# A new written-out order of all operations for a fused linear-attention and gated-unit kernel, planned with other prices for two of its operations

## The chip, the core and the metric

The kernel runs on one core of a Trainium2 chip. The time is that of one execution on the device, in microseconds (us); a kernel is run several times and the median is compared. A core has a matrix engine (TensorE, PE in the profile), two engines that can read TensorE's output memory PSUM (VectorE, DVE; ScalarE, ACT), a fourth engine that cannot (GpSimd, POOL), a queue engine that only issues transfers here (SyncE, SP), and 16 DMA engines. Each engine works through its own list of instructions in order and waits at an instruction until what it needs is there.

## The reference, cut to what matters

Inputs are q, k and v of 8 batches x 8 heads x 576 positions x 64, and four weights. Everything is float32 outside.

```python
def phi(x):
    proj = einsum('bhsd,df->bhsf', x, w_phi)            # 64 -> 128 features
    proj = proj - max(abs(proj), axis=-1)
    return concatenate([exp(proj), exp(-proj)], -1)
q_p, k_p = phi(q), phi(k)
kv  = einsum('bhsf,bhsd->bhfd', k_p, v);  z = sum(k_p, axis=2)
x   = einsum('bhsf,bhfd->bhsd', q_p, kv) / (einsum('bhsf,bhf->bhs', q_p, z) + 1e-6)
# x is put together to 8 x 576 x 512
gate = sigmoid(sum over 5 taps of conv_w[k] * x shifted by 4 - k positions)
out  = (gate * (x @ w_val)) @ w_out
```

## The kernel before, in words

The work is cut by batch, and a batch into small tasks. A position pair (two neighbouring positions of a head) makes a row of 128 numbers, so that a batch of q or k is 18 chunks of 128 such rows; they are treated in five units (UNITS) of 4, 4, 4, 4 and 2 chunks. For each batch:

* k and q are brought in and transposed. Batch 0 comes as float32 and is transposed on TensorE (tp32) and copied out of PSUM by DVE or ACT (tc32, lines 516 to 522). Batch 1 comes as bf16, is transposed on TensorE (tp16) and copied by DVE or ACT (tc16, lines 535 to 540). From batch 2 on the loads go out on GpSimd's queue (load) and a transposing DMA goes out on SP's (xpose, line 543). v comes on SP's queue (loadv, line 509) into two buffers that batches use in turn.
* For k: kp projects a unit into two PSUM banks, kmax (DVE, line 562) takes the absolute maximum, kexp (ACT, line 572, two per unit) writes the two exponentials. The maximum is not subtracted but goes as exp into v: ek (ACT) makes the factors and vs (GpSimd, line 588; one of 32 on DVE) scales v with them, four times per batch. st (36 matmuls each) sums k and v products, kv copies them out (DVE or ACT).
* For q: qm projects, qmax (DVE) takes maxima, mqt and mqr turn them round, qp projects again with the maximum subtracted, qexp (ACT, line 657) makes the exponentials.
* num multiplies q's features with kv, nrm (DVE, lines 688 to 691) divides, xtp and xtc (or a DMA, xtd) turn the result, halo (GpSimd) copies its rims. gate (TensorE) does the convolution, tanh (ACT) the gate, val (TensorE) the value product, gv (DVE) their product, gvc (GpSimd) collects left-over columns, out (TensorE) makes the output, oev (DVE or ACT) evicts it, odma (SP) stores it.
* Once, near the start: c_eb, c_cw, c_cw2 and c_gt make weights for the q projection and the gate. c_gt is 15 GpSimd instructions (lines 469 to 478) that need c_cw2 on DVE. hold is a tiny copy that keeps GpSimd's first loads until k of batch 0 has landed.
* warm2 is a pair of matmuls whose result nobody reads; NW says how many such tasks there are, and WARM puts in more of them as "place in the order : bank : how many".

The order around all this is written out. build makes the list of about 1,060 tasks, each with its engine or engines, a planned duration for each, and its needs. A planner outside the file made three strings out of that list, and follow (line 145) only reads them: ORDER is the order in which tasks are emitted, by their numbers in build; FLEX says, for each task that two engines could do, which one does it (A, D or P); BANKS gives each PSUM group its banks. An engine's list is the part of ORDER that is its own. The planned durations, dve and act among them, don't reach the program. The warm tasks have the numbers 1 to NW, so that with another NW all numbers behind them shift.

SP's queue holds the loads of v, the transposing DMAs and the stores in one order. In the first part it is: k and q of batch 0, v of batches 0, 1 and 2, then the transposition of k of batch 2.

Of the kernel before, what the change touches and what calls it, by code (L numbers as in the profile page):

```python
# [16 lines left out]
B, H, S, D = 8, 8, 576, 64  # L17
F = 128
DM = 512
P = 128  # L20
# [5 lines left out]
PEB = 1  # L26
XB = (6, 7)
NO = 6
NW = 14
NJ = 2 * NC  # L30
XH = R // 2
HALO = 16
XW = HALO + XH
WARM = (
    "8:7:5 21:7:1 214:5:1 "
)
STD = 1.18
E1 = D + 1
QW = 2 * NR

ORDER = (
    "15 16 18 17 20 19 22 21 24 35 23 37 26 25 36 39 57 27 38 59 41 32 34 170 40 43 61 60 33 172 55 42 73 74 64 47 171 174 58 "
    "193 311 49 63 44 0 28 76 62 56 50 29 48 65 93 75 45 94 67 53 91 66 54 30 46 92 51 68 97 173 31 89 98 77 188 90 184 52 "
    "185 95 194 96 69 186 189 72 79 5 187 99 228 2 71 100 229 104 313 190 105 70 226 80 9 106 227 101 78 1 103 234 191 110 "
    "175 235 192 10 111 230 178 102 182 179 183 107 112 231 180 108 195 312 11 181 232 109 84 233 81 197 203 82 206 196 6 85 "
    "113 83 314 204 198 8 7 114 199 12 201 319 236 237 205 86 200 320 115 238 202 207 87 210 4 88 116 239 208 315 14 240 118 "
    "117 316 209 211 119 122 212 128 317 241 129 215 242 123 217 124 318 214 125 120 130 213 176 131 243 321 216 329 121 13 "
    "332 3 322 126 331 177 127 132 218 324 330 354 433 434 219 323 355 247 221 248 435 139 220 352 140 353 250 141 436 252 "
    "358 359 149 222 251 249 325 437 150 133 327 356 134 357 244 438 135 246 360 361 223 326 245 333 224 439 136 225 328 137 "
    "265 335 362 266 142 138 363 334 337 143 145 144 338 336 151 339 367 152 440 369 146 253 340 370 254 441 368 267 268 255 "  # L50
    "341 259 442 372 269 256 261 343 260 364 371 443 262 147 366 444 342 148 450 365 446 447 263 452 154 449 445 451 166 155 "
    "257 264 562 448 563 258 458 565 167 344 459 453 347 485 564 345 461 273 346 274 486 454 460 348 455 270 275 477 478 162 "
    "456 271 566 481 457 158 482 163 479 272 480 376 159 349 377 160 483 284 484 378 156 462 350 161 464 285 373 465 351 157 "
    "276 374 567 463 277 487 286 466 488 568 375 467 279 278 492 569 287 379 493 280 153 380 288 281 468 570 494 282 289 164 "
    "573 283 571 577 575 391 472 578 295 576 299 392 165 296 574 393 572 579 290 469 685 686 394 300 606 470 580 607 395 381 "
    "688 471 495 687 382 385 473 496 307 386 497 608 308 581 383 583 609 387 303 584 388 489 304 384 689 291 491 582 389 490 "
    "292 498 604 390 499 474 605 475 500 585 476 610 588 405 611 399 406 690 400 586 410 407 401 691 396 587 411 501 397 612 "
    "503 414 692 613 398 502 589 402 415 591 614 403 693 408 590 404 615 293 592 616 409 593 297 510 618 595 301 506 511 168 "
    "412 617 507 294 696 413 622 298 699 729 812 813 516 730 302 624 425 416 169 594 517 504 623 814 426 421 698 505 518 619 "
    "422 519 815 508 621 697 599 512 429 620 513 727 816 430 509 628 596 629 520 431 728 731 600 630 597 694 625 732 598 735 "  # L60
    "432 627 514 736 417 626 515 712 733 418 695 715 601 734 714 700 602 702 713 521 603 524 703 522 817 527 523 701 525 528 "
    "530 526 818 529 531 704 532 737 705 708 819 537 711 738 707 539 538 820 709 535 706 305 540 633 710 427 536 739 423 716 "
    "533 634 309 740 722 306 631 534 741 748 428 632 856 750 745 424 935 857 541 643 746 635 936 310 644 639 723 747 636 542 "
    "937 640 749 751 645 637 646 753 938 558 543 638 647 752 823 559 717 854 862 641 826 863 939 546 855 825 724 718 642 547 "
    "860 725 861 554 726 824 742 555 858 744 719 859 827 720 743 828 940 651 721 648 941 652 649 662 653 650 754 829 419 663 "
    "654 548 755 830 831 556 655 832 756 942 420 656 766 549 864 833 767 760 757 557 550 834 865 943 835 761 821 768 837 660 "
    "544 769 560 551 758 770 661 838 869 759 657 870 836 822 664 944 871 866 665 658 868 762 666 763 659 867 872 545 667 979 "
    "873 839 980 764 561 677 842 945 765 874 673 678 840 981 674 780 982 843 675 771 841 850 781 679 772 985 782 774 986 552 "
    "676 773 977 775 978 950 680 776 777 844 953 954 553 778 955 785 779 952 669 786 668 951 783 845 670 956 671 789 784 957 "
    "875 672 790 849 983 877 846 984 946 847 876 787 848 949 878 788 851 880 947 962 791 879 852 965 804 853 948 963 958 987 "  # L70
    "805 883 959 964 796 988 966 884 881 960 972 893 882 887 797 894 889 961 885 888 992 973 989 994 886 890 798 895 800 896 "
    "991 891 799 808 801 993 897 968 892 974 967 990 1001 975 1002 998 976 681 1003 809 999 969 682 810 995 1000 970 907 996 "
    "971 904 908 997 905 792 811 909 1004 906 1006 1005 793 1012 1007 1010 1016 1013 1008 916 1011 898 1009 1017 1014 901 917 "
    "1018 899 902 1019 910 1015 903 794 900 1020 806 914 683 911 795 912 802 807 1024 913 684 1021 915 803 1025 1027 1026 "
    "1030 1028 1031 1022 1029 923 1032 1037 924 1023 925 1033 1039 926 1034 1035 1040 1038 927 919 928 1036 931 929 920 1041 "
    "1054 932 918 921 930 1046 933 1055 922 1058 1056 1047 934 1042 1048 1059 1062 1057 1060 1050 1043 1049 1051 1044 1063 "
    "1052 1061 1045 1053 "
)
FLEX = (
    "ADAADAAAAAPPAPPDAAAADDAADAPPDPPDDAAADPPDPPDDADAPPAPPDAAAAAPPAPPDAADDPPAPPAAADADPPDPPDDADAPDDPPADDDDA"  # L80
)
BANKS = (
    "460006544445500124166757234523230145452301456767723672301674501445674652345230145234501276045505450101236723016701016767"
    "674230145670101011236736601674501014523236503323016723674501454567232370123456723450124567741230123236745236732374567452"
    "323450123452367010016767230167676452322367450167016767453636623674567452301452301454500101010101232320101732014501676767"
    "010122154523230145674545676767454450145674545450012303223672301010145236636423236745456701010145014524523670167452323457"
    "201230145450123457466234567014567230123674545701672301672345230177674501234545016744555"
)


# [18 lines left out]
def dve(n, ov=0.075):  # L109
    return n / 960.0 + ov  # L110


def act(n):
    return n * 0.000833 + 0.067
# [42 lines left out]
def build(plan, em=None):  # L157

    def fn(name, *a):
        if em is None:  # L160
            return None
        f = getattr(em, name)
        return lambda t: f(t, *a)
# [14 lines left out]
    for b in range(B):  # L178
# [19 lines left out]
        if b:  # L198
# [24 lines left out]
            for w in "kq":  # L223
                if b <= PEB:
                    for i, (c0, n) in enumerate(((0, 8), (8, 8), (16, 2))):
                        g = plan.group("tp", 1)
                        tp = A("x" + w, b, i, "PE", 0.06 * n, fn("tp16", w, b, c0, n), [xf[w]], g, 0)
                        h.setdefault(("tps",), []).append(tp)
                        x = A("x" + w, b, i, ("DVE", "ACT"), (dve(n * P), act(n * P)), fn("tc16", w, b, c0, n), [tp], g)
                        for u, (d0, m) in enumerate(UNITS):  # L230
                            if c0 <= d0 < c0 + n:
                                h["x" + w, b, u] = x
                    continue
                dp = [G("kp", b - 2, u) for u in range(NU)] if w == "k" else [G(k, b - 2, u) for u in range(NU) for k in ("qp", "qm")]
                x = A("x" + w, b, 0, "SP", 2.7, fn("xpose", w, b), last + dp, lat=-1.5)
                last = [x]
                x = A("x" + w, b, 0, "DMA", 3.3, None, [x])
                for u in range(NU):
                    h["x" + w, b, u] = x
            h["xf", b] = xf["k"]  # L240
        if b == 1:
            g = plan.group("mqt", 1)
            cc = A("mqt", 0, 0, "PE", 0.5, fn("c_cw"), [G("kmax", 0, 4)], g, rank=-500)
            cc = A("mqt", 0, 0, "DVE", 0.2, fn("c_cw2"), [cc], g, rank=-500)
            cg = A("mqt", 0, 0, "POOL", 5.0, fn("c_gt"), [cc], rank=-10)
            for j in range(4):
                h["val", 0, j].deps.append(cx)
                h["gate", 0, j].deps.append(cg)
# [602 lines left out]
```

## Time and profile before

| what | value |
|---|---|
| median of 11 runs | 230.3 us (228.26 to 231.38) |
| the profiled execution's own time | 230.43 us |
| its span, first to last instruction | 228.6 us |
| TensorE matmul busy | 209.3 us, 4027 matmuls |
| ACT busy | 181.1 us, 266 instructions |
| DVE busy | 176.3 us, 264 instructions |
| GpSimd busy | 102.8 us, 158 instructions |
| granted TensorE clock, mean | 0.983 |
| idle matmuls (line 481) | 35, 11.2 us busy |

The profile's page has the busy share of each engine, the same in 40 slices of the span (each digit a tenth), the clock that TensorE was granted, and groups of instructions by line with busy time, mean duration of one, and the idle time ahead of them with the instruction that ended it. Beside it stand the chain of work that ended last, a table of who waited for whom, and busy times by window. TensorE's matmuls are pipelined and their ends are modelled, so its busy time is an upper bound of its work.

### The profile page before, as it was taken

The numbers are of one execution on the slowest core, as the hardware profiler recorded it, in microseconds if no ns is written. First come the engines' busy times: TensorE is split into PE (matmuls) and PEld (weight loads), VectorE is DVE, ScalarE is ACT, GpSimd is POOL, SyncE is SP. The second block draws the span as 40 slices with busy tenths as digits, with TensorE's granted clock in tenths as the row PEclk, the third lists the DMA queues.
The fourth block names the chain that finished last, engine by engine and source line by source line (L and its number), as shares of the span: only waits on it lengthen the run. The fifth ranks groups of instructions, "written<-read, shape, count | busy, mean of one in ns | idle before, by whom it ended". The sixth has DMA issues, their size and how long they took to land.

```text
span 228.6 us, 9164 instructions
## 1 busy us (share of the span) xinstructions
PE 209.3 (92%) x4027; PEld 144.3 (63%) x4027; DVE 176.3 (77%) x264; ACT 181.1 (79%) x266; POOL 102.8 (45%) x158
## 2 busy tenths in 40 slices
PE   7789998698888999989999999999999999999991
PEld 3466555566575676757677777676665876676640
DVE  2669776998679895989699979788798899483362
ACT  2888999789699988988999989979988999903320
POOL 2716993594029608930099008920119649100020
PEclk9859999999999999999999999999999999999999
DMA  6999945999598939996799998969974206166156
GB/s 207 324 259 280 208 75 147 212 176 186 96 196 232 195 91 179 287 206 79 150 216 179 265 158 231 181 127 230 274 242 143 53 3 142 37 91 202 46 171 198
DMA packets 49282, 39.87 MB, mean 174 GB/s; under 512 B 33690, under 2 KB 38554, under 8 KB 49178
## 3 DMA queue, kind: packets, MB, share of 16 engines
q1 hardware_dynamic: 43136, 29.76, 53.7%
q0 software_dynamic: 5760, 9.31, 24.2%
q8 instruction: 31, 0.51, 0.9%
q10 hardware_dynamic: 346, 0.22, 0.3%
q14 instruction: 9, 0.07, 0.1%
HBM read 30.49 MB, written 9.44 MB: 175 GB/s over the span
## 4 chain that ended last, share of the span: by engine, by line
PE 56%; DVE 21%; DMA 7%; POOL 5%; issue 4%; ACT 4%; DVEq 0%; SPq 0%; ACTq 0%
PE PS L751 13%; PE PS L775 10%; PE PS L732 7%; PE PS L555 6%; DVE MQP L562 5%; PE PS L598 5%; DVE XN L691 4%; DVE MK L562 4%; DMA kT<-KQN 4%; PE PS L670 3%; POOL VT L588 3%; PE PS L739 3%; PE PS L642 2%; DVE GV L757 2%; DMA KTIL<-in_q_dram 2%
## 5 line engine op out<-in xcount | busy, mean ns | idle before, releaser
L588 POOL TENSOR_TENSOR VT<-VN,EK 128x1152 bf16<-128x1152 f32 x31 | 65.8, 2123 | 61.3 <-ACT EK L581 50.9
L572 ACT ACTIVATE KTIL<-PS 128x1024 bf16<-128x1024 f32 (+1 forms) x80 | 72.4, 948 | 6.1 <-PE PS L555 3.9
L657 ACT ACTIVATE QTIL<-PS 128x1024 bf16<-128x1024 f32 x64 | 62.6, 1036 | 3.8 <-PE PS L649 3.3
L562 DVE TENSOR_REDUCE MQP<-PS 128x8 f32<-128x1024 f32 (+1 forms) x40 | 44.1, 1113 | 6.4 <-PE PS L555 5.2
L562 DVE TENSOR_REDUCE MK<-PS 128x8 f32<-128x1024 f32 (+1 forms) x40 | 44.0, 1112 | 2.4 <-PE PS L555 1.9
L751 PE MATMUL PS<-XT,WV 64*128 64x288 bf16 x512 | 35.4, 283 | 0.4 <-DVE XN L691 0.2
L757 DVE SCALAR_TENSOR_TENSOR GV<-TH,PS 128x576 bf16<-128x576 bf16 x32 | 23.7, 752 | 15.5 <-PE PS L751 10.8
L775 PE MATMUL PS<-WOUT,GV 128*128 128x512 bf16 x128 | 31.8, 380 | 0.0
L743 ACT ACTIVATE TH<-PS 128x576 bf16<-128x576 f32 x32 | 20.1, 654 | 13.7 <-PE PS L739 13.6
L751 PEld LDWEIGHTS <-WV 64*128 64x128 bf16 x512 | 24.6, 94 | 8.2 <-issue 2.6
L598 PE MATMUL PS<-VT,KTIL 64*128 64x65 bf16 x1152 | 24.0, 191 | 1.5 <-POOL VT L589 0.6
L598 PEld LDWEIGHTS <-KTIL 64*128 64x128 bf16 x1152 | 21.2, 95 | 4.2 <-issue 1.4
L691 DVE TENSOR_TENSOR XN<-PS,RCP 128x512 bf16<-128x512 f32 x32 | 22.1, 692 | 1.1
L670 PE MATMUL PS<-KV,QTIL 128*128 128x65 bf16 x512 | 20.1, 194 | 1.5 <-DVE GV L757 0.5
L670 PEld LDWEIGHTS <-QTIL 128*128 128x128 bf16 x512 | 18.2, 97 | 5.0 <-issue 2.7
L612 ACT ACTIVATE OUTS<-PS 128x512 f32<-128x512 f32 x22 | 13.3, 606 | 10.0 <-PE PS L775 9.1
L732 PE MATMUL PS<-XT,GF 128*64 128x288 bf16 x256 | 20.6, 290 | 0.4 <-DVE MQP L562 0.2
L720 POOL COPY XT<-XT 128x224 bf16<-128x224 bf16 x8 | 3.0, 374 | 35.2 <-DVE XT L716 22.3
L775 PEld LDWEIGHTS <-GV 128*128 128x128 bf16 x128 | 11.0, 97 | 11.6 <-issue 1.1
L555 PE MATMUL PS<-W,kT 64*128 64x128 bf16 x288 | 15.0, 220 | 2.7 <-ACT kT L522 0.9
L555 PE MATMUL PS<-W,qT 64*128 64x128 bf16 x288 | 15.4, 223 | 1.0 <-ACT TH L743 0.6
L642 PE MATMUL PS<-qT,W 64*128 64x512 bf16 (+1 forms) x80 | 15.0, 359 | 0.8 <-ACT QTIL L657 0.5
(74 smaller groups left out, 261.8 us busy)
## 6 DMA issues: line engine op xcount, KB each, us to landing
VN<-in_v_dram SPq DMA_DIRECT2D x8, 1152.0 KB, 6.7
out_dram<-OUTS SPq DMA_DIRECT2D x32, 256.0 KB, 3.5
KQN<-in_q_dram POOLq DMA_DIRECT2D x6, 576.0 KB, 6.5
KQN<-in_k_dram POOLq DMA_DIRECT2D x6, 576.0 KB, 8.4
KTIL<-in_k_dram SPq DMA_DIRECT2D x4, 288.0 KB, 4.2
KTIL<-in_q_dram SPq DMA_DIRECT2D x4, 256.0 KB, 4.6
out_dram<-OUTS SPq DMA_DIRECT2D x14, 64.0 KB, 3.2
QTIL<-in_q_dram POOLq DMA_DIRECT2D x1, 576.0 KB, 9.0
```

The lines of the kernel that those rows point to most:

```text
L555: nc.tensor.matmul(self.PS[:, t.grp.banks[par], i * P:(i + 1) * P], X[rows, (c0 + i) * P:(c0 + i + 1) * P], self.W2[rows, :], start=True, ...
L562: self.nc.vector.tensor_reduce(o, self.two(t.grp, n * P).rearrange("p a (c f) -> p a c f", f=F), AX.X, ALU.max, apply_absolute_value=True)
L572: self.nc.scalar.activation(self.KTIL[b % 2][:, s, c0:c0 + n, :, :].rearrange("p c a f -> p a c f"), self.two(t.grp, n * P).rearrange("p a ...
L588: eng.tensor_tensor(self.VT[g][:, s, :, 0:D], self.VN[b % 2][:, NC * g:NC * g + NC, :], e.to_broadcast([P, NC, D]), ALU.mult)
L598: nc.tensor.matmul(self.PS[:, t.grp.banks[ab], (s * 2 + x) * E1:(s * 2 + x + 1) * E1], self.KTIL[b % 2][rows, s, J // 2, J % 2, :], self.V ...
L657: self.nc.scalar.activation(o, i, AF.Exp, scale=1.0 - 2.0 * s)
L670: nc.tensor.matmul(self.PS[:, t.grp.banks[h // 4], (h % 4) * E1:(h % 4 + 1) * E1], Q[:, s, c % 2, h, (c // 2) * P:(c // 2 + 1) * P], self. ...
L691: nc.vector.tensor_tensor(o.rearrange("p (g h) d -> p g h d", g=ng), n[:, :, :, 0:D], rc.unsqueeze(3).to_broadcast([P, ng, 4, D]), ALU.mult)
L732: self.nc.tensor.matmul(self.PS[h2 * D:(h2 + 1) * D, t.grp.banks[par], 0:R], self.GF[:, h, i, :], X[:, h, :, HALO - 8 * s:HALO - 8 * s + X ...
L751: nc.tensor.matmul(self.PS[:, t.grp.banks[par], 0:R], self.WV2[rows, h, j * P:(j + 1) * P], X[rows, h, :, HALO:XW], start=(h == 0), stop=( ...
L757: nc.vector.scalar_tensor_tensor(out=self.GV[b % 3][:, j, :, :], in0=self.TH[j][:, :, :], scalar=1.0, in1=self.two(t.grp, R), op0=ALU.add, ...
L775: nc.tensor.matmul(self.PS[:, t.grp.banks[0], :], lhsT, self.WOUT[:, j, :], start=(j == 0), stop=(j == 3))
```

## The change

The two planned durations are changed, the number of idle pairs goes from 14 to 11, and ORDER, FLEX, BANKS and WARM are replaced as a whole. No function that emits an instruction is touched.

```diff
-NW = 14
+NW = 11
...
 WARM = (
-    "8:7:5 21:7:1 214:5:1 "
+    "9:7:5 98:5:2 "
 )
...
 ORDER = (
-    "15 16 18 17 20 19 22 21 24 35 23 37 26 25 36 39 57 27 38 59 41 32 34 170 40 43 61 60 33 172 55 42 73 74 64 47 171 174 58 "
...
+    "0 12 13 15 14 17 16 19 18 21 32 20 34 23 22 33 36 25 24 35 38 54 31 26 167 58 37 40 61 169 62 52 39 63 56 44 168 171 190 "
...
 FLEX = (
-    "ADAADAAAAAPPAPPDAAAADDAADAPPDPPDDAAADPPDPPDDADAPPAPPDAAAAAPPAPPDAADDPPAPPAAADADPPDPPDDADAPDDPPADDDDA"
+    "ADDADDADAAPPDPPDAADADDDDDDPPAPPADDDADPPDPPAAADDPPAPPADADADPPAPPADADDPPDPPADADAAPPDPPDDADADPDPPDDADADA"
 )
...
-                        x = A("x" + w, b, i, ("DVE", "ACT"), (dve(n * P), act(n * P)), fn("tc16", w, b, c0, n), [tp], g)
+                        x = A("x" + w, b, i, ("DVE", "ACT"), (dve(n * D), act(n * P)), fn("tc16", w, b, c0, n), [tp], g)
...
-            cg = A("mqt", 0, 0, "POOL", 5.0, fn("c_gt"), [cc], rank=-10)
+            cg = A("mqt", 0, 0, "POOL", 6.4, fn("c_gt"), [cc], rank=-10)
```

Read by FLEX, the tasks that two engines could do are shared out so:

| task | before: ACT, DVE | after: ACT, DVE |
|---|---|---|
| tc32 (batch 0, k and q out of PSUM) | 8, 2 | 5, 5 |
| tc16 (batch 1, k and q out of PSUM) | 3, 3 | 0, 6 |
| kv | 6, 10 | 8, 8 |
| oev | 22, 14 | 17, 19 |
| vs (GpSimd, DVE) | 31, 1 | 31, 1 |

GpSimd's list begins, before: hold; load q,1; load k,1; c_wv; load q,2; c_eb; vs; load k,2; vs; c_gt; vs; vs. After: c_eb; hold; load q,1; load k,1; c_wv; load q,2; load k,2; c_gt; and the four vs. ACT's first list differs too: before, ek of the first half of batch 0 stands ahead of the first qexp; after, it stands behind two of them. SP's list begins alike up to the first stores; later the stores stand at other places among the transposing DMAs and the loads of v. TensorE's tail, behind the last st of batch 7, has the same operations in another order, but for one out of batch 5, which stands ahead of it in the new order.

## The prediction

> **What bounds the kernel now.** I read the page's busy shares first, then the slices, the chain that ended last, the waits, and last the groups by shape for prices.
>
> ```profile
> span 228.6 us, 9164 instructions
> PE 209.3 (92%) x4027; PEld 144.3 (63%) x4027; DVE 176.3 (77%) x264; ACT 181.1 (79%) x266; POOL 102.8 (45%) x158
> ...
> PE   7789998698888999989999999999999999999991
> PEld 3466555566575676757677777676665876676640
> DVE  2669776998679895989699979788798899483362
> ACT  2888999789699988988999989979988999903320
> ...
> PEclk9859999999999999999999999999999999999999
> ```
>
> TensorE looks like the bound at 92%, but a busy TensorE includes matmuls that wait in its pipeline. Taking from the timeline the start of each operation to the start of the next, and for each kind the shortest fifth of these (val 0.98 us, out 0.86, st 0.58, a pair of gate parts 0.72), all TensorE operations sum to about 180 us. So some 43 us of the span are stretch, most of it before 80 us. ACT is at 8 or 9 tenths from the third slice to about 198 us, where the last exponential of batch 7 ends; then it is nearly empty and TensorE alone works through gates, values and outputs to 223.5 us. So there are three stages: a start (0 to 45 us) ruled by chains, a middle (45 to 198 us) in which ACT, DVE and TensorE are all near full and take turns, and a tail of 25 us that is TensorE work and the last store. In the ten windows from 100 to 200 us ACT is busy 8.46 to 10.00 of each 10, DVE 6.87 to 9.82: ACT leads by a little.
>
> The start's chain goes through GpSimd and a transposing DMA (view of the chain in order of time):
>
> ```profile
> 30.52 1.02 POOL GQ L477
> 31.54 2.08 POOL VT L588
> 33.82 2.00 POOL VT L588
> 36.41 8.97 DMA kT<-KQN
> 45.43 0.62 PE PS L555 x16
> ```
>
> The reader is to see that batch 2's key transposition starts only after the last v scaling of batch 0: on SP's queue it stands behind the load of v for batch 2, and that load waits for the buffer that those scalings read.
>
> **The change, part by part.** The two planner prices (dve(n*P) to dve(n*D) in tc16, 5.0 to 6.4 for c_gt) put nothing into the program; they matter only through the new ORDER, FLEX and BANKS. Every computing operation stays. Counted by build's numbering, the two orders say the following.
>
> *Moved between engines.* FLEX sends three tc32 copies of 512 columns (q0, q2, k2), all three ACT tc16 copies and a net five output evictions from ACT to DVE, and two KV evictions from DVE to ACT. Prices by shape:
>
> ```profile
> L612 ACT ACTIVATE OUTS<-PS 128x512 f32<-128x512 f32 x22 | 13.3, 606 | 10.0 <-PE PS L775 9.1 <-ACT KTIL L572 0.8
> L608 DVE TENSOR_SCALAR OUTS<-PS 128x512 f32<-128x512 f32 x14 | 9.5, 685 | 2.9 <-PE PS L775 2.6 <-DMA out_dram<-OUTS 0.2
> L522 ACT CAST qT<-PS 128x512 bf16<-128x512 f32 x4 | 2.4, 589 | 0.3 <-PE PS L514 0.3
> L540 ACT COPY qT<-PS 128x1024 bf16<-128x1024 bf16 x1 | 1.0, 1012 | 0.1
> L538 DVE COPY qT<-PS 128x1024 bf16<-128x1024 bf16 x1 | 0.7, 692 | 0.0
> L716 DVE COPY XT<-PS 64x256 bf16<-64x256 bf16 x16 | 4.5, 281 | 0.9 <-PE PS L703 0.6
> L606 DVE CAST KV<-PS 128x520 bf16<-128x520 f32 x10 | 7.0, 696 | 2.8 <-PE PS L598 2.8
> L610 ACT CAST KV<-PS 128x520 bf16<-128x520 f32 x6 | 3.8, 628 | 0.9 <-PE PS L598 0.8
> ```
>
> ACT loses 3 x 0.589 + 1.012 + 2 x 0.38 + 5 x 0.606 = 6.57 us and gains 2 x 0.628 = 1.26: net -5.3 (181.1 to 175.8). DVE gains 3 x 0.692 + 0.692 + 2 x 0.281 + 5 x 0.685 = 6.76 us and loses 2 x 0.696 = 1.39: net +5.4 (176.3 to 181.7). The leads are exchanged; about 3.5 us of it (ACT) and 3.3 (DVE) fall in the start, the rest in the middle. A 256-column bf16 copy on 128 partitions is not in DVE's rows; I take the 64-partition row, 0.28, bounds 0.2 and the 0.42 of an f32 copy of 256: two of them, under 0.3 us in all.
>
> *Idle matmuls.* 35 become 29 (14 pairs and 7 singles to 11 pairs and 7). At 11.2 us busy for 35 this is 6 x 0.32 = 1.9 us off TensorE. They were placed in holes before 48 us, so on the path I count 0; bounds 0 and -1.9. Their other effect is the clock. The windows show the granted clock at 0.72 from 9 to 10 us and 0.50 from 10 to 16 us, after three microseconds in which TensorE was busy 1.22 of 2.00 and 0.53 of 1.00; in that stretch a projection of eight matmuls takes 0.61 to 0.63 us, elsewhere 0.40. The single idle matmul at 6.46 us goes. From 17 us on the clock is 1.00 throughout, with TensorE above 0.79 in every window to 20 us and 0.81 in every ten after 30, idle matmuls or not. I take 0; a cold stretch longer by half (3 us at half speed, 61% of it TensorE work) would cost 3 x 0.61 x 0.5 = 0.9 us, if TensorE set the pace there.
>
> The Trainium skill, page "TensorE: Matmul & The Clock Gate", section "What's actually happening", speaks against this part: it says the clock falls to half after an idle window of about 3.4 us and comes back after as long a busy one. Its "Why this matters" section asks for no idle gaps over about 3 us. Between 4 and 12 us TensorE's idle gaps stay under 1 us and the clock fell all the same, so the rule does not fit this start by itself; by it, one more cold window would add an estimated 3.4 x 0.61 x 0.5 = 1.0 us to the sum, and one less would take as much off.
>
> *The start, walked.* DVE's new order up to c_cw2 is five tc32 (4 x 0.69 + 0.42), kmax of units 2, 0, 1, 4 and qmax of 1, 2, 4, 0 (six at a spacing of 1.14, two at 0.61), then 0.19: 11.4 us from its first copy at 5.93, so 17.3 without a wait. Before, DVE had waited 4 us by its first mqr; the new order meets PSUM banks that ACT frees by 12 to 14 us, so I allow 1.3 to 2.7: c_cw2 ends at 18.6 to 20. GpSimd then has c_gt (24.85 to 31.50 before, 6.65 us) ahead of all four v scalings (spacing 31.50 to 33.71, 2.21): 18.7 + 6.7 + 8.8 = 34.2 to 35.6, where it now ends at 36.03. It is earlier because the 2.15 us c_eb moves to the idle GpSimd ahead of hold (2.1 to 7.4 us idle), and because GpSimd no longer stands idle from 12.4 to 19.16 until v lands. ek of units 0 to 2 moves behind two exponentials of q, but it is needed only at 25.4, and I place it at 24. load k,2 is issued some ten microseconds earlier (21.36 before), while the DMA share is already 1.05 to 1.21; nobody waits for it sooner, since the transposition waits for v, and no other load stands behind it on GpSimd's queue until 47 us. So the transposition starts 0.4 to 1.8 us sooner, and batch 2 with it. On ACT, the first exponential of q comes at about 22 as now (22.17: mqr ends near 21 in both), with the same ten left to do, but three tc16 fewer in or after that stretch, and ek of batch 1 has 4.2 us less work ahead of it. I take **-1.3** for the start, bounds +1.0 (an unseen bank or DMA wait of the size of the longest in the start, 1.0) and -2.8.
>
> *The middle.* ACT loses 5.3 - 3.5 = 1.8 us, DVE gains 5.4 - 3.3 = 2.1. From 40 to 200 us ACT is busy 142.6 of 160, DVE 135.2: they become about 140.8 and 137.3, both under the leader's 142.6. If ACT's idle time stays, the middle is shorter by 1.8; if DVE's does, longer by 2.1. The nearer is ACT, the leader in 11 of the 16 windows of ten: I take **-0.9**, half of its gain. A new order may also leave more or fewer holes: the present one leaves ACT 17 us idle here, and a tenth to a fifth of that either way is 1.7 to 3.4 us. Bounds +4 and -4.
>
> *The tail.* After the last st of batch 7 the new order has one out less (out 5,0 is moved ahead of it): 0.86 to 1.04 us of TensorE in a stretch where TensorE is at 5.00 of 5.00. It has to fit into the middle instead, and the first num waits for the same exponentials. The very end keeps its chain: five outs of batch 7, the last eviction on DVE (0.69), and the store until 228.6. I take **-0.7**, bounds 0 and -1.0.
>
> Sum: 230.4 - 1.3 - 0.9 - 0.7 = **227.5 us**, against the profiled execution's 230.43 (span 228.6 and 1.8 around it). The median of the eleven runs is 230.3, so the two agree and no correction is made.
>
> **Rivals.**
>
> 1. *DVE becomes the bound (slower).* Up to mqr of batch 7 DVE has 5.5 us more work ahead of it, by the spacings of its rows (145.9 to 151.5). Mechanism: maxima come later, mqr releases the q projections later, and ACT waits. It decides if DVE cannot take the 5.5 us out of its present idle time, 35 us up to there; DVE's longest waits (10.8 us in all for val, 4.3 for tanh) can't be used for maxima if the banks aren't free. At half of it, 2.8, less the tail's 0.7 with nothing won at the start: 230.4 + 2.1 = 232.5 us. Against it: DVE is idle 52 us, and ACT's waits on DVE are small (1.8 us for MK). Chance 0.26.
> 2. *ACT sets the pace fully (faster still).* Its whole 5.3 us and the tail come out: 230.4 - 5.3 - 0.7 = 224.4 us. For it: the timeline shows ACT near full from 30 to 198 us. Against: TensorE's work in 100 to 200 us is 8.3 to 9.5 of each ten by the shortest spacings. Chance 0.14.
> 3. *No change.* The transposition's 8.97 us and the 14.8 us loads under a full DMA set the start, and the new order's holes eat the rest: 230.0 us. That the change doesn't do what it says belongs here: it plans better and the chip doesn't follow. Chance 0.15.
>
> The forecast case has 0.45. Half a per cent, 1.15 us, is about what a measurement of this kernel can tell from no change. Faster: nearly all of the forecast case and rival 2, **0.57**; same **0.16**, slower **0.27**. The range holds the bounds of the forecast, most of rival 2 and rival 1 at its price: **223.8 to 232.6**.
>
> **What would show it.** Start: GpSimd's fourth VT scaling ends before 35.6 us and the kT transposition follows; TensorE takes it up before 45.0. First ACT exponential of q near 22. Middle: ACT's busy time near 175.8, DVE's near 181.7; last exponential of batch 7 at about 196.3 instead of 198.5. Tail: about 24.5 us from there to the last matmul instead of 25.0. The forecast is wrong if DVE's waits for matmuls shrink while ACT's waits for DVE grow by microseconds (rival 1), if the clock's low stretch lasts beyond 17 us or returns, or if TensorE, free of waits, is full from 45 us on.

## The result, and the profile after

The new kernel takes 233.38 us in the median of 12 runs (231.96 to 236.36), the one before 230.39 us in 47 runs beside them: a ratio of 1.0131, 95% interval 1.0105 to 1.0157. It is slower by about 3 us; the forecast was 227.5, and the time lies above the range. The profiled execution took 232.77 us, 2.3 us more than the one before: 2.0 of them lie in the span (230.7 against 228.6), 0.3 around it. A second set of runs of the same kernel (after_again below) gave 1.0100 (1.0061 to 1.0138), with a span of 229.6.

The page of the new kernel, the lines that answer to those of before:

```profile
span 230.7 us, 9159 instructions
PE 207.6 (90%) x4021; PEld 143.1 (62%) x4021; DVE 180.8 (78%) x273; ACT 176.9 (77%) x257; POOL 102.9 (45%) x158
...
PE   6679988788989989999999899979999999899991
PEld 2446656557765667667766676847756775777640
DVE  2799897798779778998898699858798998583242
ACT  2767999998997878997898889973988999622340
...
PEclk9999999999999999999999999997999999999999
```

The engine totals are close to the forecast (ACT 176.9 for 175.8, DVE 180.8 for 181.7). The clock's hole at the start is gone, and TensorE has a new one late: the digits 7 in the PE and PEclk lines, beside a 3 of ACT. The windows of two microseconds there (columns: length, then busy time of each engine with its instructions, granted clock, DMA share, GB/s) and the timeline of TensorE show it:

```profile
152.00:154.00 2.00, 0.54 (x10) 0.20 (x6) 1.23 (x1) 1.58 (x3) 0.00 (x0) 1.00 0.11 17
154.00:156.00 2.00, 1.90 (x31) 1.29 (x32) 0.57 (x1) 1.37 (x2) 0.00 (x0) 0.70 1.55 73
156.00:158.00 2.00, 2.00 (x34) 1.80 (x35) 1.55 (x6) 0.00 (x0) 0.00 (x0) 0.50 0.20 41
```

```profile
152.24 0.29 PE L750 MATMUL PS<-XT,WV 64*128 64x288 bf16 x2
154.10 1.22 PE L750 MATMUL PS<-XT,WV 64*128 64x288 bf16 x14 [1.56 <-issue]
```

In the middle of one value product TensorE starts nothing for 1.85 us (1.56 after the modelled end; gaps are given from start to start from here on), "issue": it waited for nothing that the profile shows. Then its clock is at 0.70 and 0.50 for two windows, and ACT has little to do. In the trace's DMA records an instruction queue makes 31 fetches of 16 KB during TensorE's 8,055 instructions (matmuls and weight loads), so one for about 260 of them. The one at this gap starts at 151.77 us, 439 instructions after the last, while GpSimd's loads of q and k for batch 7 are on their way (144.4 to 153.6), and TensorE goes on 2.3 us after that start. This is called the fetch stall from here on.

**Where the time goes, in events that both kernels share.** ORDER tells which TensorE instruction belongs to which task, so the end of the last matmul of a group can be read from the timeline of any run. Between these ends lie nearly equal amounts of TensorE work: 2,274 and 2,270 matmuls up to the last state product (st) of batch 4, then 1,102 and 1,108 up to the last of batch 6, then 651 and 643. One profiled execution each, us:

| kernel | start to st of batch 4 | from there to num of batch 5 | to st of batch 6 | to the end |
|---|---|---|---|---|
| before | 129.1 | 36.3 | 18.1 | 45.1 |
| after | 128.7 | 36.6 | 20.6 | 44.8 |
| after_again | 127.9 | 36.3 | 20.6 | 44.9 |
| g_after_before | 129.3 | 36.3 | 18.1 | 45.1 |
| after_loads7_early | 129.0 | 35.1 | 20.6 | 45.0 |
| after_kp62 | 129.3 | 35.6 | 20.6 | 44.7 |
| after_both | 128.2 | 35.3 | 20.6 | 44.5 |
| after_loads7_behind | 129.5 | 35.3 | 20.6 | 45.4 |
| after_behind_kp62 | 130.1 | 35.5 | 20.6 | 44.9 |
| after_half_qmax | 127.4 | 35.3 | 20.6 | 44.8 |

The first column scatters by over 2 us from one execution to the next and is 128.9 on average over 13 profiles that begin with the new order and its allotment, and 128.9 over five that begin with the old: nothing is won by there. The end is the same within half a microsecond too. The loss in the span lies between 129 and 185 us: 54.4 us before, 55.7 to 57.2 after, for nearly the same work (59.2 in after_cut4, below). By the modelled ends TensorE is idle for 0.36 us of that stretch before; in the seven profiles of the new order and its local edits whose clock held there, it is idle for 1.1 to 2.5 us more, and the stretch is longer by 1.2 to 2.4 us. The middle two columns have to be read together: the new order has 20 matmuls fewer ahead of num of batch 5 and 26 more behind it.

The 0.3 us around the span goes with the beginning of the order: whole time less span is 2.03 to 2.16 us in every execution on record of a kernel that begins with the new order, and 1.74 to 1.87 in every one of a kernel that begins with the old, whatever follows. What takes this time the runs don't show.

TensorE's busy time by stretch, first of before, then of the new kernel (columns as above):

```profile
120.00:130.00 10.00, 9.88 (x268) 7.63 (x268) 9.82 (x15) 9.57 (x16) 6.25 (x9) 1.00 1.15 244
...
150.00:160.00 10.00, 9.95 (x239) 7.18 (x239) 8.14 (x14) 8.63 (x12) 0.00 (x0) 1.00 0.88 192
160.00:180.00 20.00, 20.00 (x347) 13.32 (x347) 16.92 (x23) 18.07 (x25) 9.71 (x13) 1.00 0.67 203
...
sum 100.00, PE 98.96 PEld 70.16 DVE 84.63 ACT 90.52 POOL 42.86; mean PE 14.14 PEld 10.02 DVE 12.09 ACT 12.93 POOL 6.12
```

```profile
120.00:130.00 10.00, 9.05 (x238) 6.39 (x236) 8.10 (x11) 8.43 (x12) 4.21 (x6) 1.00 0.95 215
...
150.00:160.00 10.00, 8.40 (x143) 6.15 (x137) 7.06 (x14) 5.39 (x7) 0.00 (x0) 0.83 0.82 110
160.00:180.00 20.00, 19.54 (x294) 12.27 (x292) 17.31 (x24) 17.40 (x25) 6.89 (x7) 1.00 0.58 152
...
sum 100.00, PE 96.03 PEld 67.70 DVE 86.30 ACT 85.41 POOL 42.68; mean PE 13.72 PEld 9.67 DVE 12.33 ACT 12.20 POOL 6.10
```

From 100 to 200 us before leaves TensorE idle for 1.04 us of 100, while ACT idles 9.5 and DVE 15.4. The new order leaves it idle for 3.97.

### The profile page after: what moved, and what is told of

Its sections match the earlier page's. It is cut to its first block, busy times and chain, and to the rows that moved or that the text cites. A ratio compares the mean times of both kernels' runs of the same rounds, so it can differ in the third digit from the quotient of the medians.

```text
span 230.7 us, 9159 instructions
## 1 busy us (share of the span) xinstructions
PE 207.6 (90%) x4021; PEld 143.1 (62%) x4021; DVE 180.8 (78%) x273; ACT 176.9 (77%) x257; POOL 102.9 (45%) x158
## 4 chain that ended last, share of the span: by engine, by line
PE 65%; DVE 14%; ACT 8%; issue 6%; POOL 3%; DMA 2%; SPq 0%; DVEq 0%; ACTq 0%
PE PS L750 14%; PE PS L774 11%; PE PS L731 7%; PE PS L554 7%; PE PS L597 7%; PE PS L669 5%; DVE MK L561 4%; ACT KTIL L571 4%; PE PS L738 3%; PE PS L641 3%; DVE MQP L561 3%; DVE XN L690 2%; DMA KTIL<-in_k_dram 2%; PE PS L648 2%; POOL VT L587 2%
## 5 line engine op out<-in xcount | busy, mean ns | idle before, releaser
L656 ACT ACTIVATE QTIL<-PS 128x1024 bf16<-128x1024 f32 x64 | 61.9, 1036 | 4.0 <-PE PS L648 3.6
L561 DVE TENSOR_REDUCE MK<-PS 128x8 f32<-128x1024 f32 (+1 forms) x40 | 44.2, 1113 | 4.7 <-PE PS L554 3.4
L561 DVE TENSOR_REDUCE MQP<-PS 128x8 f32<-128x1024 f32 (+1 forms) x40 | 44.2, 1113 | 4.5 <-PE PS L554 3.8
L750 PE MATMUL PS<-XT,WV 64*128 64x288 bf16 x512 | 36.2, 284 | 2.9 <-issue 2.1
L597 PE MATMUL PS<-VT,KTIL 64*128 64x65 bf16 x1152 | 23.3, 191 | 1.8 <-issue 0.8
L597 PEld LDWEIGHTS <-KTIL 64*128 64x128 bf16 x1152 | 20.7, 95 | 4.2 <-issue 2.1
L669 PEld LDWEIGHTS <-QTIL 128*128 128x128 bf16 x512 | 18.8, 100 | 4.8 <-issue 2.6
L611 ACT ACTIVATE OUTS<-PS 128x512 f32<-128x512 f32 x17 | 10.3, 613 | 9.3 <-PE PS L774 9.2
L731 PEld LDWEIGHTS <-GF 128*64 128x64 bf16 x256 | 13.1, 109 | 6.2 <-issue 2.1
L762 POOL COPY GVT<-GV 128x64 bf16<-128x64 bf16 x32 | 6.5, 242 | 22.8 <-DVE GV L756 22.8
L607 DVE TENSOR_SCALAR OUTS<-PS 128x512 f32<-128x512 f32 x19 | 12.9, 684 | 4.2 <-PE PS L774 3.9
```

What stands on the lines that cost most here:

```text
L561: self.nc.vector.tensor_reduce(o, self.two(t.grp, n * P).rearrange("p a (c f) -> p a c f", f=F), AX.X, ALU.max, apply_absolute_value=True)
L597: nc.tensor.matmul(self.PS[:, t.grp.banks[ab], (s * 2 + x) * E1:(s * 2 + x + 1) * E1], self.KTIL[b % 2][rows, s, J // 2, J % 2, :], self.V ...
L656: self.nc.scalar.activation(o, i, AF.Exp, scale=1.0 - 2.0 * s)
L669: nc.tensor.matmul(self.PS[:, t.grp.banks[h // 4], (h % 4) * E1:(h % 4 + 1) * E1], Q[:, s, c % 2, h, (c // 2) * P:(c // 2 + 1) * P], self. ...
L731: self.nc.tensor.matmul(self.PS[h2 * D:(h2 + 1) * D, t.grp.banks[par], 0:R], self.GF[:, h, i, :], X[:, h, :, HALO - 8 * s:HALO - 8 * s + X ...
L750: nc.tensor.matmul(self.PS[:, t.grp.banks[par], 0:R], self.WV2[rows, h, j * P:(j + 1) * P], X[rows, h, :, HALO:XW], start=(h == 0), stop=( ...
```

## The experiments

Four theories were put to the test in turn. **F**: the late instruction fetch beside the loads is the loss. **D**: VectorE, with its added work, has become the bound (rival 1 of the prediction). **P** and **C**: ScalarE starves at 150 to 160 us, alone or beside the fetch. **S**: TensorE's own order is looser in several places. Ratios are to the kernel before, with their 95% intervals.

**The same kernel again, and idle matmuls in quarters.** after_again is the new kernel unchanged. after_cut4 cuts each idle matmul in four, so that the fetches fall elsewhere:

```diff
-        self.nc.tensor.matmul(self.PS[:, bank, :], self.ONES[:, 0:P], self.ONES[:, :], start=True, stop=True)
+        for i in range(0, 512, 128):
+            self.nc.tensor.matmul(self.PS[:, bank, i:i + 128], self.ONES[:, 0:P], self.ONES[:, 0:128], start=True, stop=True)
```

> The changed kernel once more, for a second profile. Theory F (late instruction fetch): the profile of the changed kernel is 2 to 3 us ahead of the one before until 150 us and loses it all, and 2.5 us more, between 150 and 160 us, where TensorE starts nothing for 1.85 us without a wait, just when the transfer of its next 16 KB of instructions comes late (151.77 us, 439 TensorE instructions after the last one), behind the loads of q and k of batch 7; the clock then falls to 0.50 for 3 us. If that is a property of the order, the stall stands again at 150 to 156 us, over 1 us long, and the ratio is 1.010 to 1.016. Rival D (VectorE has become the bound): the loss is spread over the middle, and a second profile need not show that stall. Rival N (chance of one execution): no stall of 1 us there, with the same time.

> The changed kernel with each of its 29 idle matmuls of 512 columns cut into four of 128: the same columns, 174 more TensorE instructions before 48 us, so that the 256-instruction blocks of its program begin elsewhere in the work. Theory F: the block that came late at 151.77 is now asked for at another moment; 256 - 174 = 82 instructions later than now, about 150.5 us, when the loads are nearly done; the stall of 1.85 us and the low clock after it go, 1.8 to 3.8 us: 229.6 to 231.6 us, unless another block falls into a load. Rival D and any theory in which only the order's waits count: 233.4 within 0.5.

Measured: 1.0100 (1.0061 to 1.0138), and 1.0088 (1.0052 to 1.0123). The stall is in both: 1.06 us at 152.6 in the first, 1.99 us at 149.9 in the second, where it only moved. In the first the clock stays at 1.00 and the span is 1.1 us shorter than in the first profile of this kernel; in the second it falls to 0.50 again.

**Joining the two orders.** The first p places of one order, then what is left in the order and allotment of the other (the lines in short):

```diff
-ORDER = new
+ORDER = new[:716] + [t for t in before if t not in new[:716]]
```

> The new order up to its place 716 (about 146.5 us in its profile, ahead of the st of batch 5) with everything that is left in the old order, engines and banks by the order that each task is taken from. Theory F, and any theory that puts the loss behind 146 us: it keeps the 2.5 us lead that the new order has there and then works as the old one: 227.9 us (227 to 229). Rival D: VectorE has 3.3 us more work by there, the lead is not real time won, and the old rest takes it back: 230 to 232.

> The old order up to its place 716 and what is left in the new order. Theory F with the stall bound to the new order's rest: 2.5 us behind the changed kernel's lead and its loss as well: 234 to 236 us; if the block boundary, which lies 12 instructions earlier here, misses the loads: 231 to 232. Rival D: between the two kernels, about 232.

Measured: 1.0008 (0.9973 to 1.0042) for the new order up to place 716 (146.5 us), and 1.0176 (1.0116 to 1.0237) for the old one up to there with the new behind it. By 150 us g_after_before has lost its lead, and runs on as before does. Its time is what rival D said (230 to 232), but behind 146 us it loses nothing against before, so the new kernel's loss in the span lies behind 146 us. What the new first part is worth by itself the run doesn't tell: right behind the join TensorE stands for 1.26 us (to 150.19, waiting for a maximum on VectorE). The second join stalls too (TensorE busy 2.39 of 4 us right behind it), so that its size says little.

Four more joins were to find the place:

> The order of before up to place 866 (about 178.5 us), the new order and allotment behind it; no bank is reassigned. The join at place 716 (about 146.5 us) gave 1.0176. Theory P (the loss is made between 146 and 170 us and then only carried): the new end costs nothing, 230.0 to 231.0 us (ratio 0.998 to 1.003). Theory S (each stretch loses its own part): the stretch at 190 to 200 us and the end still cost 0.7 to 1.3 us, 231.1 to 231.8 (1.003 to 1.006). Theory E (the loss is made in the last stage alone, from 195 us on): 232 or more (1.007 or more).

> The new order up to place 872 (about 181.3 us), the order and allotment of before behind it; no bank is reassigned. The join at place 716 (about 146.5 us) gave 1.0008. Theory P (the loss is made between 146 and 170 us and carried): all of it is there, 232.3 to 233.0 us (ratio 1.008 to 1.011). Theory S (each stretch loses its own part): 150 to 160 and 170 to 180 have lost, the end has not, 231.3 to 232.0 (1.004 to 1.007). Theory E (the last stage alone): 230.0 to 230.8 (0.998 to 1.002).

> The new order up to place 760 (about 158 us), the order and allotment of before behind it; no bank is reassigned. At place 716 the same join gave 1.0008. Theory P (the stretch from 146 to 158 us, with the late fetch and ScalarE's wait, makes the loss): 1.004 to 1.009. Theory T (the loss is made behind 158 us): 0.998 to 1.003. A stall of TensorE of over 1 us within 10 us behind the join, if the trace shows one, makes the run say nothing of either.

> As the last, joined at place 804 (about 166 us); no bank is reassigned. Theory P: as at 760, 1.004 to 1.009, since from 160 to 166 us nothing more is lost. Theory T: 0.998 to 1.003, as all of it comes later (170 to 180 and 195 to 200 us). If 760 gives under 1.003 and 804 over 1.005, the loss lies between. A stall of TensorE of over 1 us within 10 us behind the join makes the run say nothing.

Measured: 1.0251 (1.019 to 1.0312), 1.0169 (1.0102 to 1.0235), 1.014 (1.0084 to 1.0195) and 1.0154 (1.0091 to 1.0217). All are slower than the new order or at its upper end, though four fifths of the first are the order that is faster. In their profiles TensorE has holes of its own right behind the join: it is idle for 2.38 us at 180 to 185, 1.49 at 180 to 190, 0.96 at 160 to 165 and 1.97 at 165 to 175; in the third a fetch stall of 2.47 us at 152.5 and a low clock stand ahead of the join. The four are inconclusive; a join is a clean cut only where both orders have done the same work.

**The loads of batch 7 moved.** GpSimd's list in the new order (early), and in the old (late):

```diff
 holdx 6
+load q 7
+load k 7
 vs 5,1,0
-load q 7
 gvc 3
-load k 7
 vs 5,0,1
```

```diff
 gvc 3
-load q 7
 vs 5,1,1
-load k 7
 halo 4
 vs 5,0,0
 vs 5,0,1
+load q 7
+load k 7
```

> The new order with one change: GpSimd issues the loads of q and k of batch 7 ahead of vs 5,1,0 instead of behind it and gvc 3, 2.2 to 2.9 us sooner (140.5 instead of 142.7 and 144.0). Theory F: the loads are through before TensorE asks for the instruction block that came late at 151.5 to 151.8 in both profiles of the new order; the fetch starts within 1.5 us of the request at about 148, the stall of 1.1 to 1.9 us at 152 is under 0.5, and the ratio to before falls from 1.010-1.013 to 1.000-1.006: 230.5 to 231.8 us. Rival D (VectorE sets the pace, the stall is only filled otherwise): same ratio, 1.010 to 1.013, whatever the stall does.

> The old order with one change the other way: the loads of q and k of batch 7 behind vs 5,0,1 on GpSimd, 6 to 8 us later (about 149.8 instead of 140.9 and 143.7). Theory F: an instruction block that TensorE asks for between 150 and 160 us comes 3 us late, TensorE stands for 1 us or more in the dense stretch around st of batch 5 or num, and the time is 231.2 to 232.5 us, ratio 1.003 to 1.008; batch 7's transposition of k, which starts at 150.2 now, would start near 160 and is needed at 172.9, so it costs nothing by itself. Rival D: 230.4, ratio within 0.3% of 1.

Measured: 1.0145 (1.0095 to 1.0194), and 1.0315 (1.0267 to 1.0364). In the first the fetch stall at 152 us is gone, and a smaller one of 0.58 us stands at 148.7, 2.2 us after the start of the fetch ahead of it; TensorE is busy 97.17 of 100 us instead of the 95.90 of after_again. The ratio is not lower for it, against theory F. The second lies far above what either theory said. In it no gap of TensorE's matmuls between 100 and 200 us is put down to issue. Instead SP's queue stands for 19.7 us at the transposing DMA that waits for k, the stores behind it wait too, and the ring of output buffers fills. The waits from 150 to 175 us and the window of 160 to 165, in before_loads7_late:

```profile
ACT OUTS L612 <- DMA out_dram<-OUTS: 4.6, 1, 4.6
...
PE PS L642 <- ACT OUTS L612: 4.0, 1, 4.0
```

```profile
160.00:165.00 5.00, 1.39 (x19) 0.73 (x14) 1.48 (x3) 0.36 (x2) 0.57 (x2) 1.00 1.20 197
```

**Order and allotment apart.** The two orders with each other's FLEX (31 tasks change engines):

```diff
 FLEX = (
-    "ADDADDADAAPPDPPDAADADDDDDDPPAPPADDDADPPDPPAAADDPPAPPADADADPPAPPADADDPPDPPADADAAPPDPPDDADADPDPPDDADADA"
+    "ADAADAAAAAPPAPPDAAAADDAADAPPDPPDDAAADPPDPPDDADAPPAPPDAAAAAPPAPPDAADDPPAPPAAADADPPDPPDDADAPDDPPADDDDA"
```

> The new order and banks with the old allotment of tasks to engines (all 31 differing tasks as before: ACT 22 output evictions, 8 tc32, 3 tc16). Rival D: VectorE loses its 5.4 us of added work and the lead on ACT comes through: faster than the changed kernel by 1 to 2.5 us, 231 us or less. Theory F: the allotment is not the cause; the stall at 152 us stays, ACT has 5.3 us more work in an order planned without it: 233 to 235.5 us.

> The old order and banks with the new allotment: ACT 5.3 us less, VectorE 5.4 us more. Rival D: slower by 1 us or more, 231.5 to 233. Theory F: the allotment is nearly neutral, 229.5 to 231.2 us.

Measured: 1.0343 (1.0279 to 1.0408) and 1.0337 (1.0283 to 1.0391). Both are far above what either theory said. Giving VectorE's added work back to ACT makes the new order 5 us slower still (1.0343 for about 1.012), and the new allotment makes the old order 7.8 us slower. The two only work together, and neither run prices the one or the other. That VectorE's share alone is the loss, so that giving it back would gain, is refuted.

**ScalarE's want at 150 to 160 us.** kp 6,2 (the third k projection of batch 6) goes directly behind val 4,1, with its exponentials; TensorE's list:

```diff
 val 4,1
+kp 6,2
 num 5,4
 mqt 6
 num 5,1
 num 5,3
 num 5,0
-kp 6,2
```

> The new order with one local edit: kp 6,2 (the third k projection of batch 6) is issued directly behind val 4,1 instead of behind num 5,4, mqt 6, num 5,1, num 5,3 and num 5,0, and its second exponential directly behind its first; it takes PSUM banks 6 and 7 (free since 152.8 us in the trace of the unchanged copy) in place of 4 and 5, which VectorE frees at 157.3. Theory P (the new order's own sequence between 150 and 160 us starves ScalarE, which was busy 6.4 us of 10 there against 8.6 before, and this costs the loss): kexp 6,2 begins at 155.7 instead of 157.7, ScalarE is busy 8 us or more of 10 between 150 and 160, the last q exponential of batch 7 ends 1 us or more sooner than 198.9, and the time falls to 231.0 to 232.0 us (ratio to before 1.002 to 1.007). Theory S (the loss is spread over several stretches, each of them a little looser than before: 150 to 160, 170 to 180, 195 to 200): at most half a microsecond comes of it, 232.2 to 232.9 (1.008 to 1.011). Theory D (VectorE's sum of work sets the pace): no gain, within 0.3 us of the copy's 232.7, as VectorE gets no less work.

Measured: 1.0135 (1.008 to 1.019). The exponentials start at 155.8 instead of 157.7, but ACT's next work, tanh 4,3, comes no sooner, and the stall is still there (1.52 us). P falls. Then both waits were taken away together:

> The new order with two edits together: GpSimd issues the loads of batch 7's q and k ahead of the fourth-last scaling of VT (vs 5,1,0), and kp 6,2 with its two exponentials runs directly behind val 4,1. Alone each was worth nothing (1.0145 and 1.0135). Theory C (two waits side by side, the late instruction fetch of TensorE and ScalarE's want of kp 6,2, each hide the other): TensorE's work left at 160 us falls by about 1 us against 56.4, and the time to 231.0 to 232.0 us where before is 230.4 (ratio 1.003 to 1.007). Theory S (the new order is as tight as its slowest chain everywhere, and VectorE's chain val 4,1 to the five normalisations sets this stretch): nothing again, 1.009 to 1.015.

Measured: 1.0083 (1.0045 to 1.0122). A fetch stall of 0.90 us stands at 147.6 us in its profile, as the fetch ahead of it now falls among the loads. The span of the profile, 228.5, is that of before, with TensorE busy 97.28 of 100 us, but over all runs the gain on the new kernel (0.2 to 0.5%) lies within the intervals. It has the lowest ratio of the new order's versions, and does not beat the old.

**The loads behind the scalings.** GpSimd issues both loads behind halo 4, and SP takes the stores first, then q, then k; once alone and once with kp 6,2 moved:

```diff
 vs 5,1,0
-load q 7
 gvc 3
-load k 7
 vs 5,0,1
 halo 4
+load q 7
+load k 7
```

> The new order with the loads of batch 7's q and k behind halo 4 on GpSimd (issued at about 147 us in place of 142.9 and 144.3), and on SP the stores of out 2,3 first, then the transposing DMA of q, then that of k (k, stores, q before). Theory F (TensorE's late instruction fetch beside the loads costs about 1 us): no gap over 0.5 us that the profile puts down to issue between 145 and 155 us, no clock below 0.9 there, and the time falls from the new kernel's 1.010 to 1.013 to 1.003 to 1.008. Theory S (the stretch is set by its order; the fetch only takes the place of another wait): 1.009 to 1.014 with the gap gone. Both fail if SP's queue or a late kT holds TensorE for over 1 us behind 160 us, which the trace would show as a wait for kT or qT.

> The same, and kp 6,2 with its exponentials directly behind val 4,1. Theory C (the two waits lie side by side and hide each other): TensorE's work left at 160 us falls below 55.5 us (56.4 in the copy of the new kernel), and the ratio to 0.999 to 1.005. Theory F (the fetch alone): as the run without that edit, within 0.3%. Theory S: 1.008 or more.

Measured: 1.0117 (1.0064 to 1.017) and 1.0107 (1.0068 to 1.0146). The condition failed: the loads' first packets go out at 148.5 us in the first, where by the count of instructions the next fetch would be due (an estimate of about 148.8), it starts at 152.2, and the gap is 1.27 us; in the second it is 1.46. So they don't take the stall away. But with it the two need 35.3 and 35.5 us from st of batch 4 to num of batch 5, and after_loads7_early, with its 0.58 us, 35.1: where the clock holds, the longer stall is worth 0.2 to 0.4 us. (after_again's 36.3 has another wait in it, 1.21 us for a kT transposition at 137.4.) Where the gap passed 1.8 us and the clock fell, the same stretch took 36.6 (the new kernel's own profile) and 38.5 us (after_cut4), 1.5 and 3.3 us more than with the small one. But F as the main cause over all executions is not borne out: in the order of the stall in their profiles, 0.58, 0.90, 1.27 and 1.46 us, the ratios are 1.0145, 1.0083, 1.0117 and 1.0107.

**Idle matmuls alone.** The old order without the pairs at 32.8, 46.0 and 46.4 us:

```diff
-NW = 14
+NW = 11
```

> The order of before with three pairs of idle matmuls fewer (29 in place of 35): those at 32.8, 46.0 and 46.4 us. Theory I (the idle matmuls fill time in which TensorE waits and keep its clock): the granted clock falls below 0.9 somewhere between 33 and 55 us and the time rises by 0.5 us or more (ratio 1.003 or more). Theory N (they are neither in the way nor needed): within 0.3% of before (0.997 to 1.003), with no clock below 0.9 there.

Measured: 1.0002 (0.9962 to 1.0041). The clock did fall, to 0.74 from 46 to 52 us, and the time did not rise: half of theory I came, without its price.

**Work taken from VectorE alone.**

```diff
-        self.amax(t, self.MQP[b % 2][:, :].rearrange("p (a c) -> p a c", a=2)[:, :, c0:c0 + n], n)
+        self.amax(t, self.MQP[b % 2][:, :].rearrange("p (a c) -> p a c", a=2)[:, :, c0:c0 + n], n, F // 2 if b in (6, 7) else F)
```

> The new kernel in which VectorE's maxima of q for batches 6 and 7 are taken over 64 of the 128 features (the rest is left out, so the output differs there): ten reductions, some 2.7 us of VectorE's work less per batch, those of batch 6 at 142 to 153 us and those of batch 7 at 167 to 183 us, and nothing else changed. Theory D (VectorE's work sets the pace of the new order, and the 4 to 6 us more that it got are the loss): the stretch from the last num of batch 5 to the last state product of batch 6 falls from 20.6 to 18.5 us or less, and the ratio to before from 1.010 to 1.013 to 1.002 or less. Theory S (TensorE's order paces it, and VectorE only runs beside): the stretch keeps 20.0 us or more and the ratio 1.007 or more. Between them, both take part.

Measured: 1.0135 (1.0087 to 1.0183). VectorE is busy for 4.6 us less from 100 to 200 us, TensorE for the same 96.07:

```profile
sum 100.00, PE 96.07 PEld 68.47 DVE 81.72 ACT 86.13 POOL 42.74; mean PE 13.72 PEld 9.78 DVE 11.67 ACT 12.30 POOL 6.11
```

The stretch from num of batch 5 to st of batch 6, where the half of this work lay, keeps its 20.6 us; theory D had 18.5 or less, and 1.002 or less. D falls: the time doesn't hang on this part of VectorE's work. The stretch is 20.56 us in eight of the nine profiles of the whole new order (20.76 in after_cut4) and in g_before_after, and 18.10 or 18.11 in before, before_idle29 and g_after_before: it goes with the order of that part, whatever came ahead of it.

## Why the prediction was wrong, point by point

Measured between the prediction's own ends in the two profiled executions, its terms are:

| term | forecast | measured |
|---|---|---|
| start, to batch 2's first k projection | -1.3 | -1.2 |
| middle, to the end of batch 7's last exponential of q | -0.9 | +2.7 |
| tail, to the last matmul | -0.7 | +0.5 |
| around the span | none | +0.3 |

They add up to the 2.3 us. In after_again the middle is +1.6 and the tail +0.3.

* **The start, -1.3: right in its steps, and worth nothing later.** The fourth scaling ended at 34.13 us (34.2 to 35.6 said), the transposition went out 1.9 us sooner, and TensorE took batch 2 up at 44.2 instead of 45.4:

```profile
31.81 2.12 POOL L587 TENSOR_TENSOR VT<-VN,EK 128x1152 bf16<-128x1152 f32 x1
33.87 0.26 POOL L588 CAST VT<-EK 128x18 bf16<-128x18 f32 x1
```

```profile
34.52 5.51 SPq L542 DMA_TRANSPOSE kT<-KQN  x1
```

  The step that failed is the one that carried this gain to the end. The state products of batch 0 end 2.2 us sooner (35.6 for 37.8), num of batch 0 only 0.4 sooner (42.9 for 43.3). ACT is busy for 8.83 of the 9 us from 34 to 43, and TensorE waits there twice for VectorE and once for ACT, 0.3 to 0.6 us each; which of them takes the lead away no run isolates. By 129 us the mean over the profiles is level.
* **The middle, -0.9: the step that failed outright.** It read ACT as the leader from busy sums of 142.6 and 135.2 of 160, and let TensorE's 99 of 100 us pass because "a busy TensorE includes matmuls that wait in its pipeline" and its shortest spacings sum to 83 to 95% of each stretch. What the runs showed in its place: ACT did lose work, it is busy for 85.4 us instead of 90.5 between 100 and 200 us, but the loss of work became idle time of ACT and no time was won. TensorE, with 1.04 us idle in the hundred, was the engine with the least room in the old order; the new one leaves it idle for 3.97, and from st of batch 4 to st of batch 6 the kernel needs 1.3 to 2.7 us more. That TensorE's idle time was the limit is an inference: its ends are modelled, and after_both has the span of before with 2.72 us idle in the hundred. The prediction's last sentence came near this ("if TensorE, free of waits, is full from 45 us on"), and the view that bears on it, TensorE's idle time by window, was there in the trace of before: from 100 us on it was all but full already. The stated bounds, +4 and -4, did hold the term.
* **The tail, -0.7: too large.** From the last exponential of q to the last matmul 25.5 us instead of 25.0 (24.5 said). From the last st of batch 7, behind which the one out is missing, to the last matmul it is 26.2 instead of 26.6 (26.0 in after_again): about half of the term came.
* **Around the span: put at nothing without a reason.** The sum kept before's 1.8 us; with the new beginning it is 2.1.
* **Idle matmuls, 0: right**, as far as before_idle29 tells, which leaves three pairs out of the old order. The clock's rise at the start (1.00 from 4 to 22 us instead of 0.50 from 10 to 16) came, and may be part of the 2.2 us that were won and lost there. Over the runs beside after_again the granted clock was 0.994 on average for the new kernel and 0.991 for the old, so the clock isn't why it is slower.
* **Engine totals and prices: right within about 1 us.** The moved evictions, copies and casts cost what the rows of before said:

```profile
L607 DVE TENSOR_SCALAR OUTS<-PS 128x512 f32<-128x512 f32 x19 | 12.9, 684 | 4.2 <-PE PS L774 3.9 <-issue 0.2
L605 DVE CAST KV<-PS 128x520 bf16<-128x520 f32 x8 | 5.6, 699 | 1.9 <-PE PS L597 1.9
L537 DVE COPY qT<-PS 128x1024 bf16<-128x1024 bf16 x2 | 1.4, 680 | 0.0
```

* **Rival 1 came near the size (232.5) by luck, with the wrong mechanism.** With 4.6 us less of VectorE's maxima nothing is gained.

**What stays open.** By shortest spacings the new order does 29.9 us of TensorE's work between st of batch 4 and num of batch 5 where the old one does 31.2, and makes up for it in the stretch to st of batch 6 (17.2 for 16.1). So about half of the 2.5 us by which that stretch is longer is work moved into it, and the time it should have saved ahead is lost in the holes there. In the other half TensorE is idle for 0.4 us more and otherwise counts as busy, and the profile names no wait of it over 0.25 us; no run isolates it. So theory S is left by exclusion, and by the stretch that keeps its length; which places of the order make the loss stays open. The cold clock behind the fetch stall is in two of the nine profiles of the whole new order; how often it comes in the timed executions the runs don't tell. That TensorE paces this part rests on its idle time, on the stretch of fixed length, and on less work for VectorE and earlier work for ACT changing nothing; no run took work from TensorE itself.

## What to carry to other kernels

Before a gain in the middle of a kernel is counted, take each engine's idle time in that stretch. Where one engine has almost none, ask what a shift of work between the others can still bring, even if its busy time is modelled: here TensorE had 1.04 us in 100, and 4.2 us less of ACT's work over the kernel brought nothing. A lead at the start counts only if it is still there at an event that both kernels share, a hundred microseconds on; compare the ends of such events, not the shares. In a written-out order that fills one engine to 99%, order, allotment and transfers hold each other up: order or allotment alone cost 3.4% here, the whole change 1.0 to 1.3%.

## What the runs showed of the hardware that was not expected

* The instruction queue made 31 fetches of 16 KB during TensorE's 8,055 instructions. Wherever a kept trace has an idle time of TensorE's matmuls of over 0.3 us put down to issue between 50 and 200 us, in the old order too (1.39 us at 58.4, 0.92 at 99.0), TensorE goes on 2.2 to 2.5 us after the start of such a fetch. The longest of these gaps, 1.85 us in the new kernel, 1.99 in after_cut4 and 2.47 in g_after_before_760, stand beside GpSimd's loads of q and k and behind a stretch in which TensorE used its instructions fast (144 st matmuls from 146.8 to 149.9 us); that the loads make the fetch late was not shown by itself.
* A gap of 1.85 us was followed by a clock of 0.70 and 0.50. The Trainium skill, page "TensorE: Matmul & The Clock Gate", section "What's actually happening", tells of an idle window of about 3.4 us before the clock falls; here TensorE was busy for 1.85 of the 3.41 us ahead of the fall (1.79 in after_cut4), and the low clock then lasted 3.41 us, from 154.81 to 158.22. Gaps of 1.06 to 1.52 us at the same place in after_again, after_kp62 and the two with the loads behind left the clock at 1.00; one of 1.99 (after_cut4) was followed by 0.85, 0.50 and 0.80, one of 2.47 (g_after_before_760) by 0.64 and 0.51.
* A transposing DMA that waits for its source held SP's queue for 19.7 us, and through the stores behind it TensorE for 4.0 us (before_loads7_late).
* VectorE copies 1,024 bf16 columns out of PSUM in 680 to 692 ns, as long as 512 float32 columns (682 to 692): the new planned price, 0.61 us, is nearer to the chip than the old 1.14, and the order planned with it is slower all the same.
